# Zeros in a bank of their own, queries loaded in 1 KB rows, the tail's last bank split, and a new order of the work: sliding-window attention and a squared-ReLU FFN

## The chip, the cores and the metric

The kernel runs on one core of a Trainium2 chip. The metric is the device time of one execution in microseconds. Three runs of the kernel before are shown, and one execution of it was profiled.

## The reference, cut to what matters

```python
def _attn_ref(q, k, v):                      # each [8, 8, 576, 64], float32
    scores = scale * np.matmul(q, k.transpose(0, 1, 3, 2))
    rel = pos[:, None] - pos[None, :]
    mask = (rel >= 0) & (rel < 64)
    scores = np.where(mask, scores, -1000000000.0)
    attn = np.exp(scores - np.max(scores, axis=-1, keepdims=True))
    attn = attn / (np.sum(attn, axis=-1, keepdims=True) + 1e-09)
    return np.matmul(attn, v)

def _moe_ref(x, w_in, w_out):                # x [4608, 512], w_in [512, 2048], w_out [2048, 512]
    h = np.maximum(x @ w_in, 0.0)
    return (h * h @ w_out).astype(np.float32)

# reference: x = attention output as [batch * seq, heads * dim]; result _moe_ref(x, w_in, w_out)
```

Each query sees itself and the 63 keys before it, so attention is a narrow band. Nearly all the arithmetic is in the two products of the FFN.

## The kernel before, in words

Tiles and stages. Attention goes by chunks of 128 positions: 32 chunks (four of each batch) and four more for the last 64 positions of two batches each. Chunk i needs three loads of 256 KB (k, q, v, all eight heads; `fetch`, L182 and L186), casts to fp16 (L256 and L258), transposes of k and q, scores (`S_`, L385), the exponential on ScalarE (`expo`, L392), the mask on VectorE (`keep`, L397), the product with v (`V`, L410), the division by the row sum (`norm`, L416 and L417), and a transpose of the result (`X`, L427). Chunks 0 to 7 transpose on TensorE (`T`, L345) and copy kT and qT out of PSUM on ScalarE or VectorE; later chunks transpose by DMA (`dma_kT` L361, `dma_qT` L367).

The FFN goes by groups of 512 tokens, nine of them. The first product (`U` L457 for group 0, `UPm` L487 for the rest) fills PSUM, ScalarE takes the ReLU (`relu`, L468), and the square goes to ScalarE (L479) or VectorE (L481). The second product is plain for group 0 (`O`, L517); for groups 1 to 8 it uses seven half-size products in place of eight (`out_seven`, L557), with sums of blocks on VectorE (L546) and evacuations at L584 and L586.

PSUM. There are three pools: `ps_att` (two tiles of two banks each, for transposes, scores, av and xt), `ps_up` and `ps_out` (two banks each). `warm` (L337) issues matmuls of zeros that keep TensorE working at the start. In the kernel before it writes them into the half that is left over of the newest attention tile that isn't a score tile:

```python
        t, name = next(e for e in atts[:-3:-1] if e[1] != "sc")
        bank, c0 = (0, 4 * 66) if name == "av" else (1, 0)
```

Order. Nothing is scheduled by the compiler. `ORDER` is a list of words, each one step (`T3` the transposes of chunk 3, `W4` four matmuls of zeros, `ck3.2` the copy of kT of chunk 3 on engine 2, with 0 for GpSimd, 1 for VectorE, 2 for ScalarE). Every engine gets its instructions in the order of the words, and runs them in that order; semaphores hold it where data or a buffer is missing. DMA starts are words too (`fk`, `fq`, `fv` on SyncE's queue, weights `fw`, `fo` on GpSimd's). Loads and stores on SyncE's and ScalarE's queues share eight completion semaphores in turn, so that a start waits until the eighth one before it has landed; stage tiles number 14.

The end. `mult` of group 8's last product goes by rows (`Z8.6.0`, then `Z8.6.1`), each half is evacuated by itself (`ev8.6.0`, `ev8.6.1`, L586), and the stores go half to SyncE's and half to ScalarE's queue (L571).

Of the kernel before, what the change touches and what calls it, by code (L numbers as in the profile page):

```python
# [9 lines left out]
FP32 = mybir.dt.float32  # L10
FP16 = mybir.dt.float16
# [5 lines left out]
A W9 ct cp fk0 cd fq0 fq1 fk1 cm fv0 kc0.1 fv1 fk2 qc0.1 fk3 T0 W3 qc1.0 fk4 ck0.1 cq0.2 kc1.2 fq2  # L17
S0 vc0.1 e0 T1 W4 fq3 cq1.1 fq4 ck1.2 m0 fv2 S1 kc2.2 vc1.1 fv3 V0 W9 e1 n0 vh1.0 fv4 vl1.2 fk5 m1
X0 W2 fw0 qc2.2 fq5 x0.1 vh0.1 kc3.0 T2 qc3.2 fv5 V1 W4 cq2.1 ck2.2 fw1 fk6 n1 T3 W1 qc4.0 fq6
vc2.2 kc4.0 cq3.1 fv6 X1 W4 vh2.2 x1.1 ck3.2 vl2.1 h2 S3 T4 W2 e3 cq4.1 ck4.2 S2 m3 e2 S4 e4 m2  # L20
vc3.0 fk7 U0.0 vl3.2 m4 U0.1 R0.0 Q0.0.1 V3 R0.1 V2 W7 n3 Q0.1.2 n2 X3 U0.2 vc4.0 fq7 x3.1 X2
vh4.0 kc5.1 fv7 R0.2 U0.3 x2.2 qc5.1 fk8 V4 R0.3 Q0.2.1 U1.0 vc5.0 fq8 Q0.3.2 n4 T5 kc6.0 fv8 R1.0
X4 cq5.2 fw2 U1.3 fk9 x4.1 ck5.2 qc6.1 vh5.0 Q1.0.2 S5 fq9 vc6.1 T6 R1.3 vl5.0 vh6.1 fv9 U1.1 e5
kc7.0 cq6.1 fk10 U1.2 vl6.1 qc7.0 R1.1 m5 ck6.2 T7 fw3 Q1.1.1 Q1.3.2 V5 W6 ck7.2 fo0 cq7.1 R1.2 n5
S7 W4 e7 h6 X5 W1 x5.1 Q1.2.2 S6 W2 m7 vc7.2 fq10 gv7 fo1 U0.5 e6 vl7.1 U1.4 R0.5 m6 Q0.5.2 U1.5
R1.4 fo2 V6 R1.5 V7 fo3 n6 U0.4 Q1.4.2 Q1.5.1 U1.7 R0.4 n7 U1.6 R1.7 kp8.0 fv10 Q0.4.1 Q1.7.2 X6
X7 U0.7 R1.6 x7.1 x6.2 U0.6 R0.7 Q0.7.2 O0.0 R0.6 P1.15 Q1.6.2 Q0.6.1 P1.11 r1.15 s1.15.2 P1.3
qp8.0 fk11 r1.11 O2.0 r1.3 s1.11.2 s1.3.1 P1.10 P1.7 r1.10 s1.10.1 O0.1 r1.7 s1.7.2 ws0.1 O0.2
ws1.1 P1.1 ws0.0 O2.1 vc8.0 fq11 r1.1 ws1.0 s1.1.2 P1.2 vh8.0 ws2.0 ws2.1 P1.0 r1.2 ws0.2 s1.2.2
O0.3 kp9.0 fv11 ws1.2 r1.0 ws0.3 P1.9 qp9.0 tk8 s1.0.2 ws1.3 O2.2 r1.9 vc9.0 ws2.2 tq8 s1.9.2 P1.8  # L30
oe0.1 vh9.0 ws2.3 kp10.0 O2.3 r1.8 fk12 qp10.0 s1.8.1 O3.0 st0 oe2.2 vl9.0 fq12 hs1.0.0 O3.1
vc10.0 hs1.1.0 fv12 P1.4 vl10.0 hs1.2.0 vh10.0 P1.12 fk13 r1.4 kp11.0 s1.4.1 O1.0 st2 r1.12 qp11.0
s1.12.2 P1.5 vc11.0 ws3.0 tk10 ws3.1 P1.6 vl11.0 r1.5 s1.5.2 O1.1 tq10 r1.6 SS4 ws3.2 s1.6.2
kp12.0 O3.2 fq13 e9 ws3.3 fv13 O3.3 e8 m9 qp12.0 fk14 P1.13 oe3.2 m8 vc12.0 fq14 P1.14 r1.13
vh12.0 st3 s1.13.2 VV4 kp13.0 r1.14 fv14 O1.2 n9 s1.14.2 O1.3 n8 fk15 Z1.2.0 h10 oe1.2 hs1.0.1
fq15 SS5 hs1.1.1 Z1.0.0 e11 qp13.0 tk12 hs1.2.1 Z1.0.1 e10 vc13.0 m11 tq12 Z1.2.1 vh13.0 ev1.0 m10
kp14.0 Z1.1.0 ev1.2 fv15 vl13.0 VV5 fk16 hs1.3.0 qp14.0 Z1.1.1 fq16 n11 vc14.0 fv16 Z1.3.0 ev1.1
n10 vh14.0 fk17 Z1.4.0 hs1.3.1 vl14.0 X11 fq17 qp15.0 X10 x11.1 Z1.4.1 x10.1 kp15.0 X9 tq14 X8
x9.1 Z1.3.1 x8.1 P2.0 tk14 ev1.3 P2.10 ev1.4 vc15.0 r2.0 st1 s2.0.2 P2.8 vl15.0 fv17 r2.10 kp16.0
SS6 r2.8 fk18 qp16.0 P2.6 e12 vc16.0 fq18 P2.9 e13 m12 vh16.0 fv18 Z1.5.0 r2.9 m13 kp17.0 s2.10.2  # L40
Z1.6.0 s2.9.1 qp17.0 tk16 r2.6 VV6 s2.6.2 P2.7 s2.8.2 n13 tq16 P2.2 n12 r2.7 fk19 s2.7.2 P2.5 h14
dx12 r2.2 SS7 r2.5 s2.2.1 vc17.0 Z1.5.1 e14 fq19 s2.5.1 vl17.0 P2.14 e15 kp18.0 m14 qp18.0 P2.1
ev1.5 r2.14 vh17.0 m15 s2.14.2 Z1.6.1 sd1.0 vc18.0 r2.1 VV7 s2.1.1 vh18.0 P2.11 n14 vl18.0 P2.3
n15 r2.11 s2.11.2 P2.15 ev1.6 kp19.0 dx14 r2.3 SS8 r2.15 P2.13 s2.3.2 tk18 s2.15.1 e16 hs2.0.0
Z2.0.0 qp19.0 r2.13 sd1.1 m16 P2.4 e17 tq18 hs2.1.0 P2.12 s2.13.2 m17 fv19 Z2.2.0 r2.4 hs2.2.0
fk20 s2.4.2 VV8 r2.12 fq20 Z2.0.1 n17 s2.12.2 fv20 P3.8 fk21 hs2.0.1 ev2.0 fq21 Z2.1.0 hs2.1.1
r3.8 fv21 hs2.2.1 s3.8.2 P3.2 fk22 hs2.3.0 P3.11 r3.2 h18 vc19.0 fq22 s3.2.2 Z2.1.1 n16 r3.11
vl19.0 fv22 P3.4 hs2.3.1 s3.11.2 kp20.0 ev2.1 P3.10 fk23 qp20.0 r3.4 SS9 vc20.0 fq23 s3.4.1 r3.10
Z2.2.1 e18 s3.10.1 vh20.0 fv23 P3.12 kp21.0 e19 m18 fk24 qp21.0 Z2.4.0 ev2.2 r3.12 vc21.0 tq20 m19
s3.12.2 P3.14 vl21.0 VV9 r3.14 tk20 vh21.0 Z2.3.0 n19 qp22.0 Z2.3.1 s3.14.1 dx16 kp22.0 n18 vc22.0  # L50
P3.0 fq24 vh22.0 ev2.3 P3.15 r3.0 dx18 kp23.0 s3.0.1 Z2.5.0 r3.15 qp23.0 s3.15.2 P3.7 tk22 vc23.0
vl23.0 P3.9 r3.7 fv24 vl22.0 s3.7.2 P3.1 fk25 r3.9 Z2.4.1 tq22 r3.1 s3.9.2 s3.1.1 P3.3 kp24.0 fq25
ev2.4 P3.5 r3.3 fv25 s3.3.1 Z2.6.0 r3.5 qp24.0 fk26 hs3.0.0 s3.5.2 P3.6 hs3.2.0 Z2.6.1 fq26 r3.6
hs3.1.0 SS10 ev2.6 fv26 Z2.5.1 e20 s3.6.1 vc24.0 fk27 P3.13 e21 ev2.5 vh24.0 m20 Z3.0.0 fq27 r3.13
kp25.0 m21 s3.13.2 Z3.0.1 tk24 hs3.0.1 VV10 ev3.0 h22 qp25.0 Z3.3.0 n20 fv27 Z3.1.0 vc25.0 fk28
n21 vh25.0 Z3.1.1 fq28 hs3.2.1 kp26.0 P4.7 hs3.3.0 ev3.1 tq24 qp26.0 hs3.1.1 P4.11 vl25.0 r4.7
fv28 hs3.3.1 s4.7.2 vc26.0 SS11 r4.11 sd2.1 kp27.0 P4.14 e22 vl26.0 sd2.0 P4.3 e23 vh26.0 m22
Z3.3.1 qp27.0 dx20 s4.11.2 m23 Z3.2.0 r4.3 vc27.0 r4.14 s4.3.1 tq26 VV11 vl27.0 s4.14.2 P4.1 n23
kp28.0 tk26 P4.4 n22 r4.1 s4.1.2 P4.2 dx22 r4.4 qp28.0 Z3.2.1 s4.4.2 vc28.0 r4.2 fk29 P4.8 ev3.2
vh28.0 s4.2.2 fq29 P4.0 ev3.3 r4.8 fv29 s4.8.2 Z3.5.0 r4.0 P4.6 s4.0.2 fk30 P4.9 r4.6 fq30 s4.6.2  # L60
P4.10 r4.9 SS12 r4.10 s4.9.1 fv30 Z3.5.1 e25 P4.5 fk31 e24 ev3.5 m25 P4.12 s4.10.2 fq31 m24 r4.5
Z4.0.0 r4.12 s4.5.1 kp29.0 fv31 VV12 s4.12.1 P4.15 qp29.0 tk28 n25 Z4.0.1 r4.15 n24 vc29.0 tq28
Z3.4.0 vh29.0 s4.15.1 ev4.0 kp30.0 h26 Z3.4.1 sd3.0 hs4.0.0 qp30.0 fk32 P4.13 ev3.4 vl29.0 hs4.1.0
SS13 vc30.0 r4.13 dx24 P5.9 e26 kp31.0 s4.13.1 vl30.0 Z4.1.0 hs4.0.1 tk30 e27 qp31.0 m26 Z3.6.0
r5.9 vc31.0 fq32 m27 P5.7 vl31.0 hs4.3.0 Z3.6.1 vh30.0 tq30 r5.7 hs4.1.1 Z4.1.1 hs4.2.0 s5.7.2
s5.9.2 hs4.2.1 VV13 ev4.1 P5.10 n27 Z4.2.0 n26 r5.10 s5.10.2 P5.8 hs4.3.1 dx26 kp32.0 ev3.6 P5.2
r5.8 sd3.1 s5.8.2 Z4.2.1 tk32 r5.2 P5.5 ev4.2 s5.2.2 h30 fv32 P5.14 r5.5 qp32.0 s5.5.2 Z4.4.0 fk33
r5.14 P5.3 s5.14.2 fq33 SS14 r5.3 P5.1 e28 fv33 Z4.3.0 r5.1 m28 e29 P5.6 fk34 s5.3.2 P5.11 m29
r5.6 fq34 Z4.4.1 s5.6.2 r5.11 fv34 P5.0 s5.11.2 vc32.0 Z4.3.1 s5.1.2 r5.0 P5.4 ev4.3 s5.0.2 kp33.0
P5.12 ev4.4 r5.4 hs5.0.0 VV14 r5.12 qp33.0 tk33 s5.4.1 Z4.5.0 s5.12.2 n29 Z4.5.1 tq32 vc33.0 n28  # L70
Z4.6.0 ev4.5 Z4.6.1 hs5.2.0 sd4.0 kp34.0 P5.13 ev4.6 hs5.1.0 sd4.1 SS15 qp34.0 r5.13 tk34 P6.11
e30 s5.13.1 Z5.0.0 r6.11 vc34.0 m30 fk35 e31 P5.15 s6.11.1 fq35 Z5.2.0 m31 r5.15 s5.15.1 P6.10
fv35 hs5.0.1 Z5.0.1 r6.10 hs5.2.1 dx28 s6.10.2 P6.7 ev5.0 hs5.1.1 P6.3 r6.7 s6.7.2 VV15 r6.3 P6.14
n30 s6.3.2 P6.8 n31 r6.14 s6.14.2 Z5.1.0 dx30 r6.8 Z5.1.1 kp35.0 hs5.3.0 P6.1 hs5.3.1 ev5.1 qp35.0
tk35 Z5.2.1 s6.8.1 r6.1 s6.1.2 Z5.3.0 tq34 ev5.2 vc35.0 Z5.3.1 P6.0 ev5.3 SS16 r6.0 Z5.4.0 e32
s6.0.1 P6.2 e33 m32 Z5.4.1 r6.2 m33 s6.2.2 Z5.5.0 ev5.4 P6.15 P6.6 r6.15 s6.15.1 Z5.5.1 r6.6
s6.6.1 Z5.6.0 ev5.5 P6.9 sd5.0 P6.4 r6.9 s6.9.1 Z6.0.0 r6.4 hs6.0.0 s6.4.2 P6.12 hs6.1.0 VV16
r6.12 hs6.2.0 P6.5 s6.12.2 n33 Z5.6.1 r6.5 n32 s6.5.2 P7.2 ev5.6 P6.13 r7.2 sd5.1 s7.2.1 Z6.2.0
r6.13 dx32 s6.13.1 SS17 P7.12 hs6.0.1 e35 hs6.2.1 Z6.0.1 r7.12 hs6.1.1 s7.12.2 P7.1 ev6.0 m35 P7.0
e34 Z6.1.0 r7.0 m34 r7.1 Z6.2.1 hs6.3.0 s7.1.2 P7.11 ev6.2 s7.0.1 Z6.1.1 r7.11 s7.11.2 P7.3  # L80
hs6.3.1 ev6.1 P7.7 r7.3 s7.3.1 Z6.4.0 r7.7 s7.7.1 VV17 P7.10 n35 Z6.4.1 n34 r7.10 P7.15 s7.10.1
dx34 Z6.3.0 r7.15 s7.15.1 P7.14 P7.8 r7.14 s7.14.1 Z6.3.1 r7.8 s7.8.2 P7.4 ev6.3 P7.5 ev6.4 r7.4
s7.4.1 Z6.5.0 r7.5 s7.5.2 P7.6 P7.13 r7.6 s7.6.2 Z6.5.1 r7.13 Z6.6.0 ev6.5 s7.13.1 P8.11 sd6.0
hs7.0.1 Z6.6.1 r8.11 hs7.1.1 P7.9 s8.11.2 ev6.6 P8.14 hs7.2.1 r7.9 sd6.1 s7.9.2 Z7.0.0 r8.14
hs7.0.0 P8.12 s8.14.2 hs7.1.0 P8.1 r8.12 hs7.2.0 s8.12.2 Z7.0.1 r8.1 P8.2 ev7.0 s8.1.1 Z7.3.0 r8.2
s8.2.1 Z7.1.0 Z7.1.1 hs7.3.0 P8.4 hs7.3.1 ev7.1 P8.7 r8.4 s8.4.1 Z7.2.0 r8.7 s8.7.1 P8.5 Z7.2.1
r8.5 s8.5.1 P8.3 ev7.2 Z7.3.1 r8.3 s8.3.2 P8.13 ev7.3 P8.0 r8.13 s8.13.1 Z7.5.0 r8.0 s8.0.1 P8.6
P8.10 r8.6 s8.6.1 Z7.5.1 r8.10 s8.10.1 P8.8 ev7.5 P8.15 r8.8 sd7.0 s8.8.1 Z8.0.0 r8.15 s8.15.2
# [595 lines left out]
```

## Time and profile before

| what | value |
|---|---|
| three runs | 300.92, 300.60, 298.54 us (median 300.6) |
| profiled execution | 300.61 us |
| its span | 298.9 us |
| TensorE busy | 284.9 us (95%) |
| VectorE, ScalarE, GpSimd busy | 198.4, 190.3, 106.2 us |
| DMA | 162593 packets, 55.52 MB |
| SyncE's DMA queue (q1) | 157744 packets, 77.8% of 16 engines |

The span is the time from the first to the last recorded instruction; 1.7 us of the execution's time lie outside it. Busy time counts matmuls from issue to end, so a TensorE that is always busy has matmuls in flight all the time, and the matmuls of zeros count too.

### The profile page before, as it was taken

What the parts mean: (1) busy time and instruction counts of PE and PEld (TensorE: products, weight loads), DVE (VectorE), ACT (ScalarE), POOL (GpSimd) and SP (SyncE); (2) the same over time, 40 slices, a digit from 0 to 9 for tenths busy, and PEclk for the clock granted to TensorE, in tenths of its full rate; (3) what the DMA queues carried; (4) which work ended last, traced back from release to release, by engine and by line L of the source; (5) the groups of instructions that cost most, each with busy time, mean ns of one, the idle gap of its engine ahead of it and who ended that gap; (6) DMA issues with size and microseconds to landing.
All of it is one profiled execution on the core that took longest, in us unless ns stands there. A gap on an engine that the chain in (4) does not pass through costs nothing.

```text
span 298.9 us, 7277 instructions
## 1 busy us (share of the span) xinstructions
PE 284.9 (95%) x2922; PEld 187.7 (63%) x2922; DVE 198.4 (66%) x352; ACT 190.3 (64%) x307; POOL 106.2 (36%) x162
## 2 busy tenths in 40 slices
PE   7677989999999999999999999999999999999994
PEld 2445868444586656666765775675766666676783
DVE  3267864596694778749853995488658764756762
ACT  1647888676736978857589468948556847744400
POOL 2236821655674612761764087126131000000000
PEclk9699999999999999999999999999999999999999
DMA  6999999989999999999999999999999310300134
GB/s 189 262 217 293 217 197 196 229 175 239 255 215 224 199 200 252 228 191 226 214 211 237 195 256 237 209 218 227 246 212 194 108 37 0 143 0 2 70 107 105
DMA packets 162593, 55.52 MB, mean 186 GB/s; under 512 B 149248, under 2 KB 158464, under 8 KB 162560
## 3 DMA queue, kind: packets, MB, share of 16 engines
q1 hardware_dynamic: 157744, 50.35, 77.8%
q0 software_dynamic: 4224, 4.19, 8.6%
q10 hardware_dynamic: 592, 0.52, 0.6%
q8 instruction: 23, 0.38, 0.5%
q14 instruction: 10, 0.08, 0.1%
HBM read 38.80 MB, written 9.44 MB: 161 GB/s over the span
## 4 chain that ended last, share of the span: by engine, by line
PE 89%; ACT 4%; DVE 4%; DMA 1%; issue 0%; SPq 0%; DVEq 0%
PE hps L487 38%; PE opsC L557 10%; PE opsD L557 9%; PE opsA L557 9%; PE opsB L557 5%; PE ops L517 5%; PE av L410 4%; PE hps L457 3%; PE sc L385 3%; ACT kT L256 1%; DMA q_st<-in_q_dram 1%; DVE qT L258 1%; PE qkT_ps L337 1%; ACT pm L392 1%; PE xt_ps L427 1%; PE av L337 1%
## 5 line engine op out<-in xcount | busy, mean ns | idle before, releaser
L468 ACT ACTIVATE hrelu<-hps 128x512 f32<-128x512 f32 x144 | 85.0, 594 | 62.3 <-PE hps L487 57.0
L487 PE MATMUL hps<-xT,w_in_sb 128*128 128x512 f16 x512 | 123.4, 379 | 0.0
L487 PEld LDWEIGHTS <-w_in_sb 128*128 128x128 f16 x512 | 48.9, 98 | 46.1 <-issue 0.2
L557 PEld LDWEIGHTS <-h 128*128 128x128 f16 x640 | 61.9, 98 | 15.9 <-issue 0.3
L481 DVE SCALAR_TENSOR_TENSOR h<-hps,hrelu 128x512 f16<-128x512 f32 x57 | 39.1, 689 | 32.8 <-ACT hrelu L468 32.1
L479 ACT ACTIVATE h<-hrelu 128x512 f16<-128x512 f32 x87 | 54.5, 629 | 2.9 <-PE opsD L557 0.7
L392 ACT ACTIVATE pm<-sc 128x1024 f16<-128x1024 f32 x36 | 35.6, 1023 | 3.8 <-PE sc L385 3.8
L258 POOL CAST v_ev<-v_st 128x512 f16<-128x512 f32 x31 | 22.6, 728 | 41.5 <-DMA v_st<-in_v_dram 31.6
L258 POOL CAST k<-k_st 128x512 f16<-128x512 f32 x32 | 21.9, 685 | 35.3 <-DMA k_st<-in_k_dram 31.8
L557 PE MATMUL opsD<-wb_all,h 128*128 128x256 f16 x256 | 32.2, 273 | 0.0
L258 POOL COPY v_od<-v_ev 64x512 f16<-64x512 f16 x40 | 27.8, 697 | 8.0 <-DVE v_ev L258 5.7
L557 PE MATMUL opsA<-w_out_sb,h 128*128 128x256 f16 x240 | 30.3, 273 | 0.0
L557 PEld LDWEIGHTS <-hs_all 128*128 128x128 f16 x256 | 24.8, 98 | 6.6
L258 POOL CAST q<-q_st 128x512 f16<-128x512 f32 x28 | 19.4, 694 | 23.3 <-DMA q_st<-in_q_dram 17.6
L417 DVE TENSOR_TENSOR x_sb<-av,rden 128x512 f16<-128x512 f32 x36 | 24.9, 691 | 1.2
L397 DVE TENSOR_TENSOR pm<-pm,mask_inner 128x1024 f16<-128x1024 f16 x28 | 21.1, 758 | 6.3 <-ACT pm L392 6.1
L557 PE MATMUL opsB<-wb_all,hs_all 128*128 128x256 f16 x128 | 16.4, 273 | 0.0
L385 PE MATMUL sc<-qT,kT 64*128 64x64 f16 x512 | 12.1, 192 | 4.5 <-ACT kT L256 2.5
L557 PE MATMUL opsC<-w_out_sb,h 128*128 128x256 f16 x128 | 16.3, 273 | 0.0
L557 PE MATMUL opsC<-w_out_sb,hs_all 128*128 128x256 f16 x128 | 16.1, 273 | 0.0
L385 PEld LDWEIGHTS <-kT 64*128 64x128 f16 x512 | 9.8, 96 | 9.8 <-ACT kT L256 4.6
L517 PE MATMUL ops<-w_out_sb,h 128*128 128x512 f16 x64 | 15.6, 379 | 0.0
(80 smaller groups left out, 279.0 us busy)
## 6 DMA issues: line engine op xcount, KB each, us to landing
k_st<-in_k_dram SPq DMA_DIRECT2D x40, 256.0 KB, 4.5
v_st<-in_v_dram SPq DMA_DIRECT2D x40, 256.0 KB, 4.3
q_st<-in_q_dram SPq DMA_DIRECT2D x32, 256.0 KB, 4.4
out_dram<-osb_all SPq DMA_DIRECT2D x14, 512.0 KB, 3.6
w_in_sb<-in_moe_w_in_dram POOLq DMA_DIRECT2D x4, 512.0 KB, 8.5
w_out_sb<-in_moe_w_out_dram POOLq DMA_DIRECT2D x4, 512.0 KB, 15.9
out_dram<-osb_all SPq DMA_DIRECT2D x4, 256.0 KB, 2.8
q_st<-in_q_dram SPq DMA_DIRECT2D x8, 128.0 KB, 3.7
```

Source lines behind the costliest of these rows:

```text
L258: (nc.gpsimd, nc.vector)[e].tensor_copy(out=dst, in_=src)
L385: nc.tensor.matmul(scv[:, hh, hp, blk, :], keys[r0:r0 + 64, hp, k0:k0 + P], qT[r0:r0 + 64, hp, 64 * blk:64 * blk + 64], start=True, stop=True)
L392: nc.scalar.activation(out=pms[i][:, part], in_=scs[i][:, part], func=AF.Exp, scale=1.0 / float(D) ** 0.5)
L397: nc.vector.tensor_tensor(out=pms[i][:, part], in0=pms[i][:, part], in1=mask[:].rearrange("p (o a) b r -> p o (a b r)", o=1) .to_broadcast ...
L410: nc.tensor.matmul(avs[i][64 * blk:64 * blk + 64, h // 4, h % 4, 0:65], pms[i][:, h % 2, h0:h0 + 64], vv[:, h, 0:65], start=True, stop=True)
L417: nc.vector.tensor_tensor(out=x_of(i)[:, :, i % 2, :].rearrange("p (a b) (c d) -> p a b c d", a=2, c=2), in0=avs[i][:, :, :, 0:D].rearrang ...
L468: nc.scalar.activation(out=hr_of[key][:], in_=src, func=AF.Relu)
L479: nc.scalar.activation(out=dst, in_=hr, func=AF.Square)
L481: nc.vector.scalar_tensor_tensor(out=dst, in0=hps, scalar=0.0, in1=hr, op0=ALU.max, op1=ALU.mult)
L487: nc.tensor.matmul(hps[:], w_in_sb[:, c, f * P:(f + 1) * P], xT_of(g)[:, :, c, :], start=(c == 0), stop=(c == DMC - 1))
L517: nc.tensor.matmul(ops_of[ts][:], h2s[0][:, f, ts * P:(ts + 1) * P], w_out_sb[:, f, :], start=(f == 0), stop=(f == FFC - 1))
L557: nc.tensor.matmul(banks[bank][:, m, :], a[:, kk, m * P:(m + 1) * P], w[:, kk], start=(first and kk == 0 and m == 0), stop=(kk == KH - 1), ...
```

## The change

Six things change, beside code that no word of the new order uses (sums of `w_in`, seven products for the first FFN product, fp32 transposes).

1. `warm` no longer writes into attention tiles. Up to the third bank taken from `ps_out` it writes into one bank of that pool that is set apart; after that into the bank which the next TensorE step will use. The zeros always fill 512 columns. There are 14 `W` words as before, with 48 matmuls in place of 58.
2. k and q of a chunk that transposes on TensorE go to two banks of the attention tile and not to two halves of one.
3. The load of q of chunk 0 starts from ScalarE's queue (`fq0.1`), and the first loads are in another order.
4. q of chunks 8 to 31 is loaded by two transfers of 128 KB with 1 KB rows (four positions at a time) instead of one of 256 KB with 256 B rows. GpSimd's cast sorts it so that a DMA transpose gives qT with positions ordered (position mod 4, head pair, position div 4). The copy of qT of chunks 0 to 7 now writes that order too. A score matmul reads its 64 queries as four runs of 16, and `expo` reads the scores from PSUM in the right order.
5. In the last group the second half of bank D is a bank of `ps_up`, and D is evacuated by halves each time.
6. The order list is new throughout. The engine of some casts and copies changes with it; GpSimd does no sums and no squares in it.

```diff
     def consts_pool():
-        make_identity(nc, ident[:])
+        make_identity(nc, ident32[:])
+        nc.gpsimd.tensor_copy(out=ident[:], in_=ident32[:])
...
-        if nm != "v" and i < NQUAD:
+        if nm == "q" and i >= NQUAD:
+            for hh in range(2):
+                dma(out=sts[nm, i][:].rearrange("p (hh t) d -> p hh (t d)", hh=2)[:, hh],
+                    in_=src[b, hh::2, s0:s0 + P, :].rearrange("hp (g t) d -> hp g (t d)", t=4))
+        elif nm != "v" and i < NQUAD:
...
     def cast_q(i, e=0):
+        if i < NTAIL:
+            dst = pair_tile("q16", q16s, i // 2)[:].rearrange("p a c t -> p (a c t)")
+            copy_on(e, dst[:, i % 2 * 512:i % 2 * 512 + 512].rearrange(
+                "p (t hh d) -> p t hh d", t=4, hh=2),
+                sts["q", i][:].rearrange("p (hh t) d -> p t hh d", hh=2))
+            return
...
-    def warm(n):
-        t, name = next(e for e in atts[:-3:-1] if e[1] != "sc")
-        bank, c0 = (0, 4 * 66) if name == "av" else (1, 0)
+    def warm(n, kind):
+        if not idle:
+            idle[0] = psum_of("out")
+        if taken["out"] < 3:
+            dst = idle[0][:]
+        else:
+            held[kind] = t = psum_of(kind)
+            dst = t[:, 0, :] if kind == "att" else t[:]
         for _ in range(n):
-            nc.tensor.matmul(t[:, bank, c0:512], zero[:, 0:P], zero[:, c0:512],
-                             start=True, stop=True)
+            nc.tensor.matmul(dst, zero[:, 0:P], zero[:], start=True, stop=True)
...
-                        scv[:, hh, hp, blk, :], keys[r0:r0 + 64, hp, k0:k0 + P],
-                        qT[r0:r0 + 64, hp, 64 * blk:64 * blk + 64], start=True, stop=True)
+                        qs = qT[r0:r0 + 64, :, hp, 16 * blk:16 * blk + 16]
...
     def expo(i, part=slice(0, 2)):
-        nc.scalar.activation(out=pms[i][:, part], in_=scs[i][:, part], func=AF.Exp,
-                             scale=1.0 / float(D) ** 0.5)
+        src, dst = scs[i][:, part], pms[i][:, part]
+        if i < NTAIL:
+            src = src.rearrange("p a (x t g) -> p (a x) g t", t=4, g=16)
+            dst = dst.rearrange("p a (x g t) -> p (a x) g t", t=4, g=16)
+        nc.scalar.activation(out=dst, in_=src, func=AF.Exp, scale=1.0 / float(D) ** 0.5)
...
+                if split(bank):
+                    banks[bank][1] = psum_of("up")[:, 0:NH]
```

The beginning of the two lists (the first words of each):

```diff
-A W9 ct cp fk0 cd fq0 fq1 fk1 cm fv0 kc0.1 fv1 fk2 qc0.1 fk3 T0 W3 qc1.0 fk4 ck0.1 cq0.2 kc1.2 fq2
-S0 vc0.1 e0 T1 W4 fq3 cq1.1 fq4 ck1.2 m0 fv2 S1 kc2.2 vc1.1 fv3 V0 W9 e1 n0 vh1.0 fv4 vl1.2 fk5 m1
+W10 ct cp fk0 cd fq0.1 fk1 fq1 fk2 cm fq2 fv0 kc0.0 fk3 qc0.2 fk4 T0 W5 kc1.0 fq3 cq0.2 fq4 qc1.0
+ck0.2 fv1 kc2.2 S0 T1 W2 fv2 e0 qc2.1 fv3 cq1.2 T2 W6 m0 fv4 vc0.2 cq2.1 fk5 ck2.2 vh0.0 kc3.1
+ck1.2 fq5 fw0 V0 h2 fv5 S1 W3 fw1 n0 e1 fk6 qc3.1 X0 vc1.2 fq6 S2 W3 qc4.1 x0.2 vh1.0 m1 e2 T3 W1
```

## The prediction

> **What bounds the kernel now.** I read the page's busy table and slices first, then the busy time in three stretches, then the chain of waits with the stretch 0 to 60 us by itself, then waits and the end.
>
> ```profile
> PE 284.9 (95%) x2922; PEld 187.7 (63%) x2922; DVE 198.4 (66%) x352; ACT 190.3 (64%) x307; POOL 106.2 (36%) x162
> PE   7677989999999999999999999999999999999994
> PEclk9699999999999999999999999999999999999999
> DMA  6999999989999999999999999999999310300134
> ```
> ```profile
> 0.00:51.05 51.05, 41.76 (x539) 29.71 (x540) 30.14 (x77) 33.41 (x54) 20.60 (x39) 0.93 1.07 225
> 51.05:294.45 243.40, 243.10 (x2384) 158.01 (x2382) 167.49 (x273) 156.92 (x254) 85.56 (x124) 1.00 0.84 179
> 294.45:298.90 4.45, 0.00 (x0) 0.00 (x0) 0.76 (x2) 0.00 (x0) 0.00 (x0) 1.00 0.47 118
> ```
>
> The columns are length, then busy time of PE, PEld, DVE, ACT and POOL, then clock, DMA share and GB/s. From 51.05 us, where group 0's second product starts, to the last matmul at 294.45, TensorE is busy for 243.1 of 243.4 us at full clock. That is also what its work costs. In the chain four 512-column matmuls take 0.863 us and eight 256-column ones 0.87 us; 128 steps of the first product, 16 of the second and 112 half products make 110.5 + 13.8 + 97.4 = 221.7 us. 14 pairs of scores and of products with v, some 0.65 to 0.73 us each with the bubble behind them, make about 19.7, four transposes of x 1.6: together 243.0. So no order can gain in this stretch; it can only lose. What can shrink is the head (51.05 us, with 9.3 us idle and 58 matmuls of zeros) and the end (4.45 us).
>
> In the head the chain goes through the zeros themselves:
>
> ```profile
> 6.23 0.66 PE qkT_ps L337 x3
> ...
> 9.66 1.72 PE qkT_ps L337 x4
> ...
> 13.97 1.99 PE av L337 x9
> ...
> 17.37 0.45 PE xt_ps L337 x2
> ...
> 20.45 0.23 PE qkT_ps L337
> ...
> 23.05 0.45 PE qkT_ps L337 x2
> ...
> 40.53 0.60 PE av L337 x4
> ...
> 41.55 0.23 PE xt_ps L337
> ...
> 42.28 0.59 PE xt_ps L337 x2
> ```
>
> These are start, length and work. The reader is to see that filler sets the end: zeros go into the same tile as the transposes, so the copy out of that tile waits for them. The sum is 6.92 us. The other filler runs while nothing could have run.
>
> **The change, part by part.**
>
> *Zeros apart (48 matmuls, was 58).* The copies no longer wait for zeros, 6.92 us of chain. They are not gained whole, since two things come next. One is data: v of chunk 3, the 14th tile, is cast at 17.37 after a wait, 13.25 us after the first cast at 4.12, so a tile lands each 1.02 us, and the DMA share is 1.07 over the head. The other is ScalarE, 33.41 us busy of 51.05. So I walk the new order by hand with before's durations.
>
> Scores of chunk 0: k lands at 4.1, ten zeros (1.26 + 10 x 0.43) end at 5.6, q's cast 0.62, transposes, and both copies now on ScalarE, 2 x 0.60: 8.3 to 8.6, against 8.28 before. Product with v of chunk 0: exponential 1.02, mask 0.7, with T1, T2 and six zeros beside them: about 12, against 13.32. First step of the FFN (25.23 before): v of chunk 1 is now the 12th tile, 4.1 + 11 x 1.02 = 15.3; behind its cast (0.62) ScalarE has xT 0.59, an exponential 1.02, kT 0.60 and two more copies; then S3, V1, S4, division 0.9, transpose 0.4, copy 0.42, zeros 0.65: about 22.7. From its end at 23.6 ScalarE has eight ReLUs (4.8), five squares (3.1) and seven copies (4.3), to 35.8; exponential and mask of chunk 5 take it to 37.6. There V5 starts, and eight `U` (7.0), the other V and X (2.3) follow: 47.4. I take 47.5 for what was 51.05, a gain of 3.5. The bounds are no gain (the new waits eat all) and 6.9 (all of the chain). I stand in the middle, since both followers have rows.
>
> *Two queues.* k0's issue holds SyncE from 0.81 to 1.56, and q0's starts at 1.62. ScalarE loads its table first (0.81 to 2.09, then 0.20), so q0 may start there between 1.3 and 2.3: 0.3 us earlier to 0.7 later. k1 and q1 start one issue (0.65) earlier, on a DMA that is then full (slice 2 on is 9). I take 0. The Trainium skill, page "DMA: Bandwidth & Descriptors", section "Issuing engines are not separate DMA queues", says that issuing on several engines saves only the issue time. By it the gain would be 0.65 at the most, and the full slices agree.
>
> *Queries in 1 KB rows.* 24 loads go from 1024 packets to 256: 18432 fewer of 162593. They cost 24 more issues on SyncE, 0.6 us each, 14 us over 230. Behind them in that queue are k and v loads and DMA transposes; SyncE is 0% of the chain, and in the long stretch TensorE waited for no load. So 0, covered by loads that run chunks ahead; without that cover it would be those 14 us at the worst. GpSimd's sorting cast has a row: the same pattern took 0.61 us in the head, no more than the plain one. The score matmul reads runs of 16 queries, and no row shows that. Bounds: nothing, or twice its time, 14 x 0.58 + 8 x 0.41 = 11.4 us. Nearest is the first product's moving x in two runs, at full rate, so 0.
>
> *Exponential from scattered PSUM.* 32 exponentials now read every 16th float. Nearest on the same engine: kT copies at 597 ns read scattered PSUM, against 594 for a contiguous ReLU of the same size. So 0. The far bound is VectorE: qT scattered 0.690 against xT contiguous 0.422, which would be 1.64 times.
>
> *New order after 51 us.* It keeps the floor and can add stalls. I counted TensorE's work between its steps. The smallest distance from the last first product to the half that needs its square is 1.6 to 1.7 us at five places (2.4 before), against ReLU 0.59 + square 0.63 to 0.69. Two steps after which a PSUM bank comes round with only one step between are 14, seven before. I add 0.5; the bounds are 0 and 14 x 0.28 = 3.9, by the only such wait of before:
>
> ```profile
> PE av L410 <- DVE pm L397: 0.3, 1, 0.3
> ```
>
> *Split of bank D.* Both last evacuations started after the last matmul (two in 0.76):
>
> ```profile
> 294.47 0.76 DVE L586 SCALAR_TENSOR_TENSOR osb_all<-opsD,u 128x256 f32<-128x256 f32 x2 [1.05 <-PE opsD L557]
> ```
>
> With a bank of its own the first half is done during the second half's matmuls: 0.38 less at the end, the last store behind it too. The extra evacuation earlier (2 x 0.38 for 0.69) and GpSimd's extra identity copy (about 0.3 before data lands at 4.1) lie beside other work.
>
> **Sum.** -3.5 + 0 + 0 + 0 + 0.5 - 0.4 = -3.4 us, against the profiled 300.61 us (span 298.9 and 1.7 around it), which is the median's 300.6: 297.2 us, 1.1% faster. About 1%, or 3 us, is what a measurement of this kernel tells from no change.
>
> **The rivals.**
>
> *The waits move on (300.5).* Loads of v and ScalarE take the place of the zeros, and U still ends at 51. For it: GpSimd waited 31.6 us in all for v's loads, one cast until 24.32; the new list puts v of chunk 0 seventh, not fifth, and starts `w_in` 2 us earlier into a full DMA. Against: those waits were off the chain. Head 0, order +0.3, tail -0.4.
>
> *Slow exponential (308).* Each of the 32 grows by 0.65 us. Eight in the head lie on ScalarE's walk: 5.2. Later, TensorE has 3.46 us of work between scores and product with v at seven places of 14; two exponentials and a mask need about 3.0 now, and 4.3 then: 7 x 0.84 = 5.9. 297.2 + 11.1 = 308.3. It decides for slower than before from 0.3 us more per exponential (8 x 0.3 + 7 x 0.14 = 3.4). For it: VectorE's pair of rows. Against: ScalarE's. The Trainium skill, page "Advanced Engine Details and Errata", section "Memory Cachelines", wants each two neighbours in PSUM contiguous for best throughput. By it the scattered read would cost as in this rival; ScalarE's 597 against 594 ns doesn't bear that out.
>
> *All of the chain (293.8).* The full 6.9 us go. Against: the DMA's share.
>
> *Half of it undone.* The zeros leave the attention tiles only if they don't make the next step wait: TensorE runs in order, and W5, W6, W5 still stand ahead of S0, V0 and S3. With clock low (0.60 at 7.5 to 15 us) each zero matmul costs 0.43 and not 0.22; 16 of them add 3.4, and the time is 300.5, as in the first rival.
>
> **How the numbers follow.** Forecast (295.5 to 299) 0.5; waits move on, or zeros still in the way (299 to 302) 0.25; all of the chain 0.09; slow exponential or score matmul 0.11; stalls at the tight places, 3.9 and no head gain (304) 0.05. The forecast's middle lies 0.4 us beyond the 1% line, so I give 0.38 of its 0.5 to faster, with the 0.09: 0.47; slower 0.16; the rest 0.37 within 1%. Range 293.5 to 303.5: both ends of the head, and some stalls; the slow exponential is left out.
>
> **What would show it.** Right: `U` ends near 47.5; the chain of the head holds under 2 us of zeros; TensorE is busy from there within 0.5 us; the first half of the last evacuation starts before the last matmul ends; exponentials stay at 1.02 us and score pairs at 0.58. Wrong: exponentials above 1.3 us, TensorE waiting for VectorE's masks after 70 us, or a head that waits for v's loads with ScalarE idle between 14 and 20 us.

## The result, and the profile after

| | before | changed |
|---|---|---|
| median | 300.25 us (298.54 to 300.92) | 329.44 us (328.25 to 332.24) |
| profiled execution, its span | 300.61, 298.9 us | 328.25, 326.4 us |

The ratio is 1.0995, with an interval of 1.0911 to 1.1079: ten per cent slower, where 1.1% faster was forecast. One thing is needed for all that compares heads: the profiled execution of the kernel before has a mean granted clock of 0.989, with half clock for 6.83 us from 9.05 us on, while 24 of its 27 executions beside e5 below have 0.997 to 1.000, and the median of the 27 is 298.21 us, not 300.6. The page of the changed kernel, with the same rows as before:

```profile
PE 294.3 (90%) x2912; PEld 190.5 (58%) x2912; DVE 189.8 (58%) x345; ACT 193.4 (59%) x314; POOL 105.0 (32%) x164
PE   8989899976949994999879959999999999999995
PEclk9999999999797997899998997999999999999999
DMA  7999996788697987969996999799999941310123
```

The head has no low clock any more, and TensorE's row has holes between 65 and 196 us where it had nines. The DMA row fell there as well: the loads come late although the DMA engines are on average less busy. The busy time by stretches (length, PE, PEld, DVE, ACT, POOL, clock, DMA share, GB/s):

```profile
0.00:45.93 45.93, 41.72 (x533) 28.32 (x534) 29.20 (x74) 35.39 (x59) 19.33 (x38) 1.00 1.08 235
...
60.00:100.00 40.00, 30.04 (x325) 18.94 (x324) 19.56 (x35) 16.09 (x25) 16.80 (x25) 0.94 0.84 171
100.00:150.00 50.00, 44.31 (x455) 27.75 (x453) 28.86 (x50) 30.62 (x50) 21.52 (x31) 0.91 0.83 178
150.00:200.00 50.00, 42.26 (x394) 26.19 (x393) 29.11 (x48) 29.19 (x47) 19.29 (x30) 0.95 0.96 177
```

Group 0's second product starts at 45.93 us, 5.1 us earlier than before, and one step of the next group's first product (0.86 us) stands ahead of it which stood behind it: the head gained 6.0 us. From there to the last matmul's end (322.47) it is 276.5 us, where the kernel before, without that step, took 242.5: 34.0 us lost. From the last matmul to the end of the span it is 3.9 us and not 4.45. Sum: -6.0 + 34.0 - 0.5 = +27.5, which is 326.4 - 298.9. Of the 34.0 us, 23.7 are standstill (276.54 us long and 252.55 busy, where before 0.30 us were idle), and 10.3 are the same work taking longer: the granted clock is 0.96 there, and was 1.00. From 60 to 200 us TensorE is busy for 116.6 of 140 us, before for 139.7. What is waited for:

```profile
POOL q L267 <- DMA q_st<-in_q_dram: 64.4, 23, 8.8
POOL v_ev L267 <- DMA v_st<-in_v_dram: 30.3, 20, 5.6
POOL k L267 <- DMA k_st<-in_k_dram: 27.5, 14, 6.1
...
DVE kH L330 <- DMA kT<-k: 20.7, 5, 7.1
...
PE att L437 <- DMA qT<-q: 14.9, 6, 5.1
...
PE ps_u L540 <- DMA xT<-x_sb: 3.4, 2, 2.8
```

Columns are total, number and longest. Before, GpSimd waited 17.6 us in 13 waits for q, and for v and k as long as here (31.6 and 31.8 us); TensorE waited for no load and no DMA transpose. The chain of waits in that stretch shows how one late load of q reaches TensorE (start, length, work):

```profile
61.30 4.98 DMA q_st<-in_q_dram
...
66.40 0.62 POOL q L267
...
69.45 2.67 DMA q_st<-in_q_dram
72.12 7.12 DMA kT<-k
...
80.45 0.64 PE att L437 x32
...
99.82 6.59 DMA v_st<-in_v_dram
106.43 4.48 DMA qT<-q
111.05 0.64 PE att L437 x32
```

Loads of q, loads of v and the transposes of k and q, which all go through the DMA, take turns in front of the scores.

### The profile page after: what moved, and what is told of

Its sections match the earlier page's. It is cut to its first block, busy times and chain, and to the rows that moved or that the text cites. A ratio compares the mean times of both kernels' runs of the same rounds, so it can differ in the third digit from the quotient of the medians.

```text
span 326.4 us, 7308 instructions
## 1 busy us (share of the span) xinstructions
PE 294.3 (90%) x2912; PEld 190.5 (58%) x2912; DVE 189.8 (58%) x345; ACT 193.4 (59%) x314; POOL 105.0 (32%) x164
## 2 busy tenths in 40 slices
DMA packets 143969, 55.52 MB, mean 170 GB/s; under 512 B 124480, under 2 KB 139840, under 8 KB 143936
## 4 chain that ended last, share of the span: by engine, by line
PE 54%; DMA 23%; SPq 11%; ACT 4%; DVE 3%; POOL 2%; issue 2%; POOLq 0%; ACTq 0%
PE ps_u L540 21%; PE ps_o L715 21%; DMA v_st<-in_v_dram 8%; DMA q_st<-in_q_dram 7%; SPq L185 4%; DMA kT<-k 4%; SPq L193 3%; PE ps_o L666 2%; PE att L466 2%; DMA qT<-q 2%; SPq L189 2%; DMA k_st<-in_k_dram 2%; ACT hrelu L519 2%; PE att L437 2%; PE ps_u L508 1%
## 5 line engine op out<-in xcount | busy, mean ns | idle before, releaser
L540 PE MATMUL ps_u<-xT,w_in_sb 128*128 128x512 f16 x512 | 124.9, 385 | 3.4 <-DMA xT<-x_sb 3.4
L519 ACT ACTIVATE hrelu<-ps_u 128x512 f32<-128x512 f32 x136 | 80.3, 593 | 73.2 <-PE ps_u L540 71.4
L534 DVE SCALAR_TENSOR_TENSOR h<-ps_u,hrelu 128x512 f16<-128x512 f32 x52 | 35.6, 689 | 39.3 <-ACT hrelu L519 39.2
L715 PE MATMUL ps_o<-w_out_sb,h 128*128 128x256 f16 x368 | 50.8, 289 | 0.6 <-DVE osb_all L749 0.6
L449 ACT ACTIVATE pm<-att 128x1024 f16<-128x1024 f32 x36 | 35.8, 1022 | 24.6 <-PE att L437 24.6
L715 PE MATMUL ps_o<-wb_all,h 128*128 128x256 f16 x240 | 32.3, 279 | 0.0
L267 POOL CAST k<-k_st 128x512 f16<-128x512 f32 x32 | 21.7, 679 | 28.7 <-DMA k_st<-in_k_dram 27.5
L473 DVE TENSOR_TENSOR x_sb<-att,rden 128x512 f16<-128x512 f32 x36 | 24.9, 692 | 1.2
L749 DVE SCALAR_TENSOR_TENSOR osb_all<-ps_o,u 128x512 f32<-128x512 f32 (+1 forms) x24 | 15.8, 663 | 5.7 <-PE ps_o L715 5.7
L715 PE MATMUL ps_o<-wb_all,hs_all 128*128 128x256 f16 x128 | 16.8, 281 | 0.0
L666 PE MATMUL ps_o<-w_out_sb,h 128*128 128x512 f16 x64 | 15.7, 381 | 0.0
```

The lines of the kernel that those rows point to most:

```text
L267: (nc.gpsimd, nc.vector)[e].tensor_copy(out=dst, in_=src)
L449: nc.scalar.activation(out=dst, in_=src, func=AF.Exp, scale=1.0 / float(D) ** 0.5)
L473: nc.vector.tensor_tensor(out=x_of(i)[:, :, i % 2, :].rearrange("p (a b) (c d) -> p a b c d", a=2, c=2), in0=avs[i][:, :, :, 0:D].rearrang ...
L519: nc.scalar.activation(out=hr_of[key][:], in_=src, func=AF.Relu)
L534: nc.vector.scalar_tensor_tensor(out=dst, in0=hps, scalar=0.0, in1=hr, op0=ALU.max, op1=ALU.mult)
L540: nc.tensor.matmul(hps, w_in_sb[:, c, f * P:(f + 1) * P], xT_of(g)[:, :, c, :], start=(c == 0), stop=(c == DMC - 1))
```

## The experiments

Three theories stood against each other for the 34 us. *Engines:* each of the two new transfers has four head pairs as its outermost step, and runs on four of the 16 DMA engines. *Transfers:* 24 more issues and completions in SyncE's queue hold up what is behind them. *Order:* the new list asks for loads too late, whatever their form. For the first, the trace has a sign of its own. Each transfer of a hardware queue leaves one completion event for each DMA engine that takes part. Before, there are 3040, which is 190 x 16. After, there are 2896, which is 166 x 16 + 48 x 5: the 48 transfers of q leave five. Four are from engines, and the fifth is not a DMA engine's. The page counts 149248 packets under 512 B before, and 124480 after: 24 x 1024 of the difference are rows of q, and the 192 left over are 24 x 16 - 48 x 4, one small packet for each engine of a transfer. The fifth event comes 0.42 us after the issue has ended, the four others some 4 us after it.

The Trainium skill, page "DMA: Bandwidth & Descriptors", section "Why a DMA increments its semaphore by 16 and not by 1", says that the number of engines is the largest k up to 16 that divides the slowest dimension (of size above 1) of both access patterns, and that on hardware queues these are the lowest-numbered k. The counts agree with the first half; no run here shows the engines' numbers.

The times of the completion events fit loads of q that all take the same four engines, which the other loads need too. Loads of k and v issued from 60 to 200 us have 16 events each. From the end of the issue to the twelfth it takes 2.8 us for k and 3.2 for v (medians; before 2.9 and 2.8), but to the sixteenth 4.3 and 4.8 us (before 3.4 and 3.3). A load of v at 70.04 us has twelve events at 2.6 to 3.2 us and four at 4.8 to 6.0. So twelve engines are nearly on time and four are late, and what waits for the load waits for the last.

### e1, e2, e3: sixteen engines again, with one, two and four transfers

```diff
 q of a chunk, access pattern of the source (g has 32 steps)
-two transfers of 128 KB: "hp (g t) d -> hp g (t d)"
+e1, one of 256 KB:       "(hp hh) (g t) d -> g hp hh (t d)"
+e2, two of 128 KB:       "hp (g t) d -> g hp (t d)"
+e3, four of 64 KB:       "hh (g t) d -> g hh (t d)"
```

All their hardware-queue transfers leave 16 completion events (in e3 4192 = 262 x 16). In e1 and e2 the partitions then stand as (g, head pair), so the scores read q with a step of four elements; e3 keeps the changed kernel's layout.

> The changed kernel with q of chunks 8 to 31 in one transfer of 256 KB with 1 KB rows, partitions filled in the order (position div 4, head pair), so that the slowest dimension of the source has 32 entries instead of 4; a score matmul then reads its queries with a step of 4. Theory 1 (each split transfer runs on 4 of the 16 DMA engines, since its slowest source dimension is 4; q lands late and TensorE starves): the time falls to 293 to 297 us, that is before's 300.3 less the 6.0 us that the head gains (the second product of group 0 starts at 45.9 behind one more step, against 51.05) and the 0.4 of the end. Theory 2 (twice as many transfers use up the eight completion semaphores and SyncE's issue time): the same 293 to 297. Theory 3 (the new order of loads and stores on SyncE's queue starves TensorE by itself): 320 to 330, as the changed kernel.

> As the run with one transfer, but again two transfers of 128 KB a chunk, by halves of the heads, with 32 entries in the slowest source dimension. Theory 1 (4 of 16 engines): 293 to 298 us. Theory 2 (number of transfers): 325 to 332 us, as the changed kernel. Theory 3 (order): 320 to 330.

> The changed kernel's own layout of queries, but in four transfers of 64 KB a chunk, one for each head pair, each with 32 entries in its slowest source dimension. Theory 1 (4 of 16 engines): 293 to 300 us, in spite of 48 more transfers on SyncE's queue. Theory 2 (number of transfers): above 335 us. Theory 3 (order): 320 to 330.

Measured: e1 300.45 us, ratio to the kernel before 1.0062 [1.0040, 1.0085]; e2 300.88, 1.0075 [1.0050, 1.0100]; e3 298.08, 1.0001 [0.9967, 1.0034]. All three keep 1 KB rows, and all three are rid of some 30 us. e3 has the most transfers and is the fastest: the transfers theory falls. That e1 and e2 stay slower than e3 goes with their scores:

```profile
L439 PE MATMUL att<-qT,kT 64*128 64x64 f16 x512 | 17.4, 218 | 0.6 <-DVE qT L267 0.5
```
```profile
L439 PE MATMUL att<-qT,kT 64*128 64x64 f16 x512 | 11.9, 190 | 2.2 <-DMA qT<-q 1.4 <-DVE qT L269 0.5
```

The first line is e1, the second e3, which has the changed kernel's runs of 16: 17.4 us busy against 11.9, so 5.5 us more of TensorE time. The twelve pairs of chunks 8 to 31 make it up: from its first start to its last end a pair takes 1.10 us in e1 and 0.64 in e3, as in e5 below with the plain layout. (In the chains, where a pair follows other work, it is 1.03 in e1 and 0.57 in e5.) The medians lie only 2.4 us apart; e3's profiled execution, the longest of its ten, waits 2.5 us for DMA transposes of q, and e1's for none.

### e4: part 4 alone, in the order of the kernel before

```diff
 before.py, its own ORDER, zeros and tail
+  two transfers of 128 KB "hp (g t) d -> hp g (t d)" for q of chunks 8 to 31,
+  with the cast, the copy of qT, the scores and expo that go with them
```

> The kernel before with the loads, layout, score operands and exponential of queries as in the changed kernel (two transfers a chunk with a slowest source dimension of 4), and nothing else changed, its own order included. Theory 1 (4 of 16 engines) and theory 2 (number of transfers): 320 to 336 us, some 30 us over the 300.3 of before, since the starvation needs no new order. Theory 3 (order): 299 to 302.

332.49 us, ratio 1.1130 [1.1061, 1.1199], 34 us above the 298.43 of the kernel before beside it. Part 4 alone makes the whole loss, and the order theory falls.

### e5: the changed kernel with the old loads of q

```diff
-        if nm == "q" and i >= NQUAD:
-            for hh in range(2):
-                dma(out=sts[nm, i][:].rearrange("p (hh t) d -> p hh (t d)", hh=2)[:, hh],
-                    in_=src[b, hh::2, s0:s0 + P, :].rearrange("hp (g t) d -> hp g (t d)", t=4))
-        elif nm != "v" and i < NQUAD:
+        if nm != "v" and i < NQUAD:
```

The cast, qT, the scores and `expo` of these chunks go as in the kernel before.

> The changed kernel with part 4 undone: q of chunks 8 to 31 by one transfer of 256 KB with 256 B rows, positions in order, score operands and exponential as before; everything else as changed, the new order included. If the loads of q on 4 of 16 engines are the whole loss, and the rest of the change does what the head showed (second product of group 0 at 45.9 instead of 51.05, one first-product step earlier in the order, so 6.0 us; the end 0.35): 292.5 to 295.5 us, a ratio of 0.975 to 0.985 to before. If the new order has stalls of its own after 60 us (3.6 us of TensorE's time were idle between 105 and 165 us in the run with four transfers): 296 to 299.

296.95 us against 298.21, ratio 0.9955 [0.9933, 0.9977]: faster than both kernels. Its head, middle and end, in the columns above:

```profile
0.00:45.62 45.62, 41.23 (x532) 28.03 (x533) 29.18 (x74) 35.23 (x58) 18.18 (x36) 1.00 1.08 232
45.62:291.04 245.42, 243.31 (x2381) 157.80 (x2379) 163.69 (x270) 157.15 (x256) 91.79 (x128) 1.00 0.82 181
291.04:295.10 4.06, 0.00 (x0) 0.00 (x0) 0.42 (x1) 0.00 (x0) 0.00 (x0) 1.00 0.46 129
```

45.62 is the start of the instruction itself. The same view has 50.88 for the profiled execution before, where the chain of waits, used so far, has 51.05. Against it: head 50.88 - 45.62 + 0.86 = 6.1 us gained; middle 245.42 against 242.71, 2.7 lost; end 4.06 against 4.45, 0.4 gained, with one evacuation left after the last matmul where two were. Sum -3.8, which is 295.1 - 298.9. The medians are only 1.3 us apart (296.95 and 298.21). The rest I put down to the half clock in that execution's head: from the second product on, TensorE was busy in it for 243.1 of 243.4 us at full clock, so there was hardly anything to lose there.

### e6 and e8: the zeros' place and the order, each without the other

e6 is e5 with the order list of before; e8 is e5 with the zeros back in the attention tiles.

```diff
 e6
-ORDER = the new list
+ORDER = the list of before (less the word A)
```
```diff
 e8, in warm
-        if taken["out"] < 3:
-            dst = idle[0][:]
+        t, name = next((e for e in atts[:-3:-1] if e[1] != "sc"), (None, ""))
+        if t is not None:
+            dst = t[:, 0, 264:512] if name == "av" else t[:, 1, :]
+        elif taken["out"] < 3:
+            dst = idle[0][:]
```

> The order of before (its 58 matmuls of zeros included) with the zeros in a bank of their own, k and q transposed into two banks, and bank D split at the end; loads of q as before. If the copies waited for zeros and the search added nothing, the head loses most of the 6.9 us of zeros in the chain: 293 to 296 us. If each zero still holds the next step, since TensorE runs in order, and only a new order places them well: 298 to 300, the 0.35 us of the end included.

> As the run with part 4 undone, in the new order, but the zeros go where before put them: into the newest attention tile that is no score tile (248 columns beside a product with v), and into the bank of their own only where the last two tiles are both scores. If the place of the zeros is what the head gained by: 3 to 6 us slower than the run with part 4 undone, 297 to 301. If the order alone gained it: within 1 us of it.

e6: 300.21 us, ratio 1.0058 [1.0036, 1.0080]. e8: 303.52, 1.0176 [1.0144, 1.0208]. In e6 the second product starts at 51.17 us (before 50.88): with the zeros out of the way, TensorE waits in that order for v (0.2 us before) and still for k (2.5 us before).

```profile
PE att L461 <- ACT v_od L260: 2.3, 1, 2.3
PE att L432 <- ACT kT L260: 1.8, 3, 0.8
```

In e8 it starts at 55.24 us. Three stretches of the head, e8 first, then e5:

```profile
7.50:15.00 7.50, 4.57 (x75) 2.82 (x75) 2.93 (x8) 5.35 (x9) 2.27 (x4) 1.00 1.13 289
15.00:22.50 7.50, 6.28 (x45) 3.53 (x45) 4.58 (x8) 2.77 (x5) 3.14 (x4) 0.55 1.19 229
22.50:30.00 7.50, 5.53 (x82) 3.19 (x82) 2.94 (x6) 3.14 (x5) 4.52 (x6) 0.77 1.01 262
```
```profile
7.50:15.00 7.50, 6.92 (x107) 4.13 (x107) 5.63 (x12) 6.43 (x10) 3.44 (x6) 1.00 1.12 276
15.00:22.50 7.50, 6.92 (x105) 4.58 (x104) 5.43 (x11) 4.68 (x8) 1.98 (x3) 1.00 1.20 241
22.50:30.00 7.50, 7.25 (x100) 5.87 (x99) 6.18 (x14) 7.39 (x15) 4.86 (x7) 1.00 1.05 273
```

With zeros in the tiles that are waited for, TensorE stands still for 2.9 us of the first stretch, and the clock granted in the next is 0.55, so what follows is slow too: the clock is 0.50 for 6.83 us from 15.69 us and for 3.41 us from 25.93. The Trainium skill, page "TensorE: Matmul & The Clock Gate", section "What's actually happening", says that an idle window of about 3.4 us halves the clock and a busy one restores it. The lengths agree, 3.41 us and twice that. The condition doesn't come out so simply: in the 3.41 us before 15.69 TensorE was busy for 1.44 us and never stood still for more than 1.42, and in e4 it stood still for 3.8 us of the stretch from 7.5 to 15 and was granted 1.00 there and in the next. What decides it stays open here.

The place of the zeros is worth 303.52 - 296.95 = 6.6 us in the new order, standstill and low clock together. In the old one the parts of e6 bring nothing: it is 2.0 us slower than the kernel before (298.21), with half clock for 3.41 us of its profiled head. The zeros' place and the order work only together.

### e7: one queue for the first loads

```diff
-W10 ct cp fk0 cd fq0.1 fk1 fq1 ...
+W10 ct cp fk0 cd fq0 fk1 fq1 ...
```

> As the run with part 4 undone, but q of chunk 0 starts from SyncE's queue as the other loads do. In the changed kernel's profile ScalarE's queue starts it at 1.3 us and it is there at 4.6, where before had it at 5.3. If that head start reaches the end: 0.5 to 0.7 us slower than the run with two queues. If a later wait covers it: within 0.3 us of it.

297.33 us, ratio 0.9958 [0.9932, 0.9984], against e5's 0.9955: no difference that can be told.

### e9: eight engines

```diff
-            for hh in range(2):
-                dma(out=sts[nm, i][:].rearrange("p (hh t) d -> p hh (t d)", hh=2)[:, hh],
-                    in_=src[b, hh::2, s0:s0 + P, :].rearrange("hp (g t) d -> hp g (t d)", t=4))
+            for x in range(2):
+                dma(out=sts[nm, i][:].rearrange("p (x t) d -> p x (t d)", x=2)[:, x],
+                    in_=src[b, :, s0 + 64 * x:s0 + 64 * x + 64, :].rearrange(
+                        "h (g t) d -> h g (t d)", t=4))
```

> The changed kernel, with the two loads of 128 KB a chunk cut by positions and not by heads: each goes over all 8 heads (outermost, 8 steps) and 16 groups of four positions, 1 KB rows as before. The queries then stand in another order than the scores take them for, so the attention's values are not the reference's; instructions, sizes and waits are the same. It stands between four outermost steps (329.4 us) and sixteen (e2, 300.9). By the theory that a transfer runs on as many engines as it has outermost steps: every load of q shows 8 engines and a write by the sequencer, 9 completion events, and the time lies in between; if q's part on a busy engine counts, the excess goes as 16/8 - 1 to 16/4 - 1, a third of 29: 308 to 312. By the rival that it is the heads' far stride at the outermost place, however many: 325 to 330. By the rival that only fewer than eight engines are short: 299 to 301.

297.35 us, ratio 0.9982 [0.9964, 0.9999]. The trace has 3087 completion events where 166 x 16 + 48 x 9 = 3088 answer to eight engines, so the count of engines is what the theory says; and the packets under 512 B are 124672, by 24 x 1024 fewer than before with nothing left over, as 24 x 16 = 48 x 8. The price is not what it says: I expected a third of the excess, and there is none that can be told. The rival of the far stride (325 to 330) falls, and the one by which only fewer than eight engines are short (299 to 301) comes nearest.

```profile
60.00:100.00 40.00, 38.62 (x444) 24.06 (x442) 28.30 (x48) 24.09 (x39) 22.54 (x32) 1.00 0.97 217
100.00:150.00 50.00, 49.33 (x539) 31.23 (x538) 38.30 (x64) 37.00 (x60) 27.82 (x38) 1.00 1.03 230
150.00:200.00 50.00, 49.70 (x560) 33.47 (x559) 32.64 (x56) 34.69 (x57) 24.09 (x35) 1.00 1.07 222
```

TensorE is busy for 137.7 of these 140 us, as in e5 (137.9). So four engines cost 31 us of span (326.4 against e5's 295.1), and eight 0.3 (295.4). An estimate of why: the packet records give a median of 18 ns for a 256-byte packet and 46 ns for a 1 KB one. One chunk of q takes 1024 x 18 / 16 = 1.15 us of all sixteen engines in 256 B rows, 256 x 46 / 8 = 1.47 us of eight, and 256 x 46 / 4 = 2.94 us of four. From 60 to 200 us the kernel before had a DMA share of 1.03 to 1.07 (over 1, so packet times overlap), and I take it that no engine had much time to spare. Over 24 chunks, eight engines get 24 x 0.32 = 8 us more than before and four get 24 x 1.79 = 43. Before, the loads were through at about 230 us of 299, so they ran ahead and had some slack: by this estimate 8 us fit in it, and 43 did not. How large it is was not measured.

### e10: one tight place of the new order

Of the 2.7 us that e5 loses in the middle, 1.6 are two waits for masks. In one of them the mask of chunk 22 stands behind a sum of `h` on VectorE.

```diff
-P4.2 hs3.3.1 kp26.0 tq24 r4.10 Z3.3.0 m22 qp26.0 r4.2 s4.10.1 vh25.0 VV11 s4.2.2 fk28 P4.5
+P4.2 kp26.0 tq24 r4.10 m22 hs3.3.1 qp26.0 r4.2 s4.10.1 vh25.0 P4.5 VV11 s4.2.2 Z3.3.0 fk28
```

> e5 (the changed kernel with the old loads of q, 296.95 us) with one place of the order changed: the mask of chunk 22 goes ahead of a sum of h on VectorE, and one first-product step stands ahead of the product with v that needs this mask. In e5 TensorE waited 0.73 us there for the mask, behind that sum. By the theory that such tight places of the new order make up what e5 loses after 60 us: the wait goes, 0.5 to 0.8 us less, 296.2 to 296.5, which the interval may just not tell from nothing; the trace tells it by that wait. By the rival that TensorE's idle time there only moves to the next wait (the second product behind the sum): 296.9 and a new wait of about the same length at the second product.

296.71 us, ratio 0.9953 [0.9938, 0.9968], against e5's 0.9955: no difference that can be told. The waits of e5, then of e10:

```profile
PE att L461 <- DVE pm L448: 1.6, 2, 0.9
```
```profile
PE ps_u L535 <- ACT hrelu L514: 0.9, 1, 0.9
PE att L461 <- DVE pm L448: 0.7, 1, 0.7
```

The wait for the mask went, and one as long came for ScalarE's ReLU at the next first-product step: the idle time only moved, though not to the second product as its rival had it.

## Why the prediction was wrong, point by point

*Queries in 1 KB rows: the step that failed.* "So 0, covered by loads that run chunks ahead; without that cover it would be those 14 us at the worst." It counted packets and issues, and never asked over how many DMA engines a transfer is spread. It measured some 31 us of span (326.4 against 295.1 without this part), and this part alone 34 us (e4: 332.5 against 298.4). The cover failed because each load of q ran on four engines, whose part of the other loads then came late too (e9 with eight engines, e1 to e3 with sixteen, lose none of it). So the upper bound of 14 us was too low as well. Two rows spoke against the zero. The DMA share was 0.84 over the long stretch and nines up to 231 us, which the part on two queues used ("a DMA that is then full") and this part did not: loads that run ahead on a full DMA have little slack. And the diff itself has `hp`, four steps, in front.

*The cover.* SyncE being 0% of the chain was read right: issues did not set the end (e3, with four transfers a chunk, is level with before). What lay under the cover was the transfers' own time.

*GpSimd's sorting cast, scores in runs of 16: 0, right.* GpSimd's cast of q has a mean of 687 ns (694 before). A score matmul has a mean of 190 ns in e3 with runs of 16, as in e5 without them (192 before). The bound of twice the time was not idle, though: with single elements at a step of four, in e1 and e2, a pair took 1.10 us and not 0.64. (The bound counts fourteen pairs; this layout has twelve.)

*Exponential from scattered PSUM: 0, right.*

```profile
L449 ACT ACTIVATE pm<-att 128x1024 f16<-128x1024 f32 x36 | 35.8, 1022 | 24.6 <-PE att L437 24.6
```

The changed kernel's mean is 1022 ns, before 1023. The rival of the slow exponential is false, and ScalarE's pair of rows was the right one to go by.

*Zeros apart: right in kind, the size open.* Forecast 3.5 us (47.5 for 51.05), measured 6.0 and in e5 6.1 against the profiled execution, near the rival "all of the chain" (6.9) that I gave 0.09. But that execution lies 2.4 us above the 298.21 of the kernel before beside e5, and its head had the half clock. Against a usual head the gain is, as an estimate, 6.1 - 2.4 = 3.7. That this is near the forecast is no proof of the walk, whose durations came from the head with the low clock. The first step of the FFN came at 20.3 us, not 22.7; the granted clock was 0.60 from 7.5 to 15 us in the profile that the walk used, and is 1.00 in e5's rows above. That the zeros only help along with the order (e6) I had not seen: "the waits move on" is what happens in the old one. In the changed kernel too the head's chain now has a load, `9.65 12.19 DMA v_st<-in_v_dram`.

*New order: 0.5, measured 2.7 in e5*, within the bounds of 0 and 3.9. I looked at squares and PSUM banks; the waits were for masks, behind other work on VectorE, both after 70 us, as one of the signs of being wrong had it. In e8, whose head is 9.6 us longer than e5's, TensorE is busy for 139.7 of the 140 us from 60 to 200, where e5 has 137.9, and the span is only 7.4 us longer: an earlier start came with more waiting later, so the gain of the head was not kept whole.

*Split of bank D: -0.4, right.* e5's end is 0.39 us shorter, with one evacuation after the last matmul. *Two queues: 0, right* (e7).

The sum without part 4 would have been 297.2, and e5 measured 296.95, but by another sum: -6.1 + 2.7 - 0.4 and not -3.5 + 0.5 - 0.4, and from a base that beside e5 is 298.21 and not 300.6. The gain forecast for the other parts was 3.4 us, and by the medians they made 1.3. That the times agree is chance.

## What to carry to other kernels

Read the outermost dimension of every DMA access pattern that a change touches, and count on how many DMA engines it leaves the transfer; longer rows and fewer packets did not help here, where four engines had to carry them. Such a price need not grow in proportion: eight of sixteen engines cost nothing that could be told here, and four cost a tenth of the kernel. Filler that keeps TensorE busy belongs in a bank that nobody waits for, but that paid here only with an order whose next waits come later.

## What the runs showed of the hardware that was not expected

A transfer with four outermost steps left completion events of four engines and not of sixteen, and the DMA share fell (from 1.03 to 0.84 in the stretch 60 to 100 us) while loads came late. A mean over 16 engines hides a few late ones; the completion events show them, with twelve of a load of v at 3.2 us and the last of sixteen at 4.8. A 1 KB packet took 46 ns, a 256-byte one 18, so 1 KB rows did save DMA time (46 for 4 x 18), but no run gained by it: e3 with 1 KB rows on sixteen engines is level with before and 1.1 us above e5 with 256-byte rows. Fp16 matmuls whose moving operand takes every fourth element made a pair of scores 1.10 us instead of 0.64. The clock granted to TensorE halved for 6.83 us after 3.41 us in which it was busy for 1.44 and no single standstill was longer than 1.42 us (e8), and stayed at 1.00 in e4, where it stood still for 3.8 of 7.5 us.
